# Turning float64 weights into float32 by scaling and shifting, and loading the first of them first

## The chip, the core and the metric

The kernel runs on one core of a Trainium2 chip. A core has five engines that work side by side, each with an instruction queue of its own that it works off in order: TensorE (PE in the profile; its weight loads are PEld) multiplies matrices into PSUM, VectorE (DVE) and ScalarE (ACT) do elementwise work, GpSimd (POOL) does elementwise work on SBUF, and SyncE (SP) here only issues DMA transfers. The metric is device time in microseconds, the median of several executions. Everything here is one core, one launch.

## The reference, cut to what matters

```python
# B, H, S, D = 8, 8, 576, 64; window 128
scores = q @ k^T / 8 + slope[h] * -(i - j)        # only for 0 <= i - j < 128, otherwise -1e9
attn   = softmax(scores);  x = attn @ v           # x: [8, 576, 512], heads side by side
theta  = x @ w_theta
zr, zi = x * cos(theta), x * sin(theta)
y      = w_tok_r @ zr + w_tok_i @ zi              # over the 576 tokens
u      = x + y
out    = u + max(u @ w_ch, 0)
```

q, k and v are float32. The weights w_theta, w_tok_r, w_tok_i and w_ch are float64: float32 draws divided by the square root of a dimension, which gives numbers of double precision. [...] A float64 has 1 sign bit, 11 exponent bits and 52 mantissa bits; the high word holds the sign, the exponent and the first 20 mantissa bits, the low word the other 32.

## The kernel before, in words

**Batches.** Everything is done batch by batch. For one batch (8 heads, handled as 4 pairs of heads) `attend` computes the windowed attention into `x_sb`, `turn` transposes x and computes theta, its cosine and sine and the products z, `mix` multiplies z with the token weights (wtok, 27 matmuls for each of 8 output pieces, line L536), and `channels` multiplies u with w_ch (L557) and writes the output. The attention of batch b+1 runs beside the mixing of batch b, which is what keeps TensorE busy in the long middle of the kernel. Products that need more precision than TensorE gives in one pass are done as a high part and a low part (`kh`/`kl`, `qh`/`ql`, `wth_hi`/`wth_lo`, `wtk_hi`/`wtk_lo`, `wch_hi`/`wch_lo`).

**The first stage.** Batch 0's attention has no mixing beside it. It is done by `start`, which also loads and converts all weights: 4 blocks of w_theta (512 columns), 9 blocks of the token weights (576 columns) and 4 blocks of w_ch (512 columns), 17 in all, each [128, columns] of float64. Its loop has five turns; in turn p it makes the scores of pair p (`Pair.scores`, L351 and L365 on TensorE, L380 on VectorE, the exponent L383 on ScalarE) and finishes pair p-1: `flip` transposes the scores (L388) and copies them (L391), `values` multiplies them with v (L424), `finish` divides (L430 to L433). `fill` issues matmuls whose results nobody reads (L569). `prepare(p)` splits q and k of pair p-1 into high and low parts (`split_pair`: kh L300 and qh L297 on ScalarE, ql L298 on VectorE, kl L301 on GpSimd) and loads pair p. `head.ready()` loads v for four heads at the first of them (`load_plain`, L218, 650 KB), and `measure_first` (L276 on VectorE) takes the largest |v| of such a group.

**The weights.** `unpack` is a generator: each `next` issues one stage of one block, and `pace` calls it three times for every five steps of the scores; what is left is issued after the loop. A block's stages are: `load` (L139) into one of four buffers (two of `big`, two of `uf`), `apart`, `together`, `split`. A buffer is taken again when its block has been split. `apart` masks the high word into the exponent bits (L149) and into the mantissa bits with the hidden one (L151), both on VectorE, and ScalarE's Relu turns the exponent bits into those of a float32 power of two (L153). `together` puts the sign on the power (L158), adds the low word times 2^-32 to the mantissa as a float32 (L160), both on VectorE, and GpSimd multiplies the two (L162). For token weights it also takes the sum of absolute values of each row (L165 on ScalarE) and a power of two from it (L166, L121, L123). `split` writes the scaled high part on ScalarE (L175, L179, L182) and the low part on VectorE (L176, L183) or GpSimd (L180).

**What sets the order.** The order of the instructions on each engine isn't the order of the code: when the kernel is built, a planner times all instructions with a model of its own and places them by priority, which is mostly the order in which the code issues them, as soon as its model says that their inputs and buffers are there. Some streams get other priorities (`urgent`, with MIX, CHAN and ROTATE) and some instructions are tied behind others (`issue_after`). The order found is then fixed; on the chip each engine works its own list off in order and waits where an input isn't there yet. All DMA transfers of this kernel are issued from SP's list.

At the end of `start`, `scales_first` computes scales for z from the row sums and the largest |v|; then pair 4's scores are made, and `turn` of batch 0 begins.

Of the kernel before, what the change touches and what calls it, by code (L numbers as in the profile page):

```python
# [11 lines left out]
F32 = mybir.dt.float32  # L12
F32R = mybir.dt.float32r
I32 = mybir.dt.int32
U32 = mybir.dt.uint32
F16 = mybir.dt.float16
BF16 = mybir.dt.bfloat16
AF = mybir.ActivationFunctionType
ALU = mybir.AluOpType
# [30 lines left out]
def attn_moe_kernel(ctx: ExitStack, tc: tile.TileContext, qt, kt, vx, wth, wtok, wch, band, out):  # L50
    nc = tc.nc
    PSUM = bass.MemoryType.PSUM

    const = ctx.enter_context(tc.tile_pool(name="const", bufs=1))
# [37 lines left out]
    scales = fixed[:, 130:134]  # L92
    bands = const.tile([128, 704], F32, name="bands")
    bnd = bands[:, :256]
    rebias = const.tile([128, 1], F32, name="rebias")
    make_identity(nc, ident)
    nc.vector.memset(halfpi, math.pi / 2)
    nc.sync.dma_start(out=bands, in_=band)
    nc.vector.memset(ones, 1.0)

    for g in range(H // 2):
# [7 lines left out]
    wtk_lo = const.tile([128, 9, S], F16, name="wtk_lo")  # L109
    sums, rows, invs, lim = (rings[name].take() for name in ("sum", "row", "inv", "lim"))  # L110

    nc.vector.memset(rebias, -float(916 << 23))
    qr = const.tile([128, S + 64], F32, name="qr")
    for t in [qr] + peaks + lasts:
        nc.gpsimd.memset(t, 0.0)
# [15 lines left out]
    def unpack(jobs, places):  # L131
# [10 lines left out]
        def words(k, t):  # L142
            w = jobs[k][4]
            raw = t[:, :2 * w].rearrange("p (n t) -> p n t", t=2)
            return raw, t[:, 2 * S:2 * S + w], t[:, 3 * S:3 * S + w]

        def apart(k, t):
            raw, ex, ma = words(k, t)
            nc.vector.tensor_scalar(out=ex, in0=raw[:, :, 1], scalar1=0x7FF00000, scalar2=None,  # L149
                                    op0=ALU.bitwise_and)  # L150
            nc.vector.tensor_scalar(out=ma, in0=raw[:, :, 1], scalar1=0xFFFFF, scalar2=0x100000,  # L151
                                    op0=ALU.bitwise_and, op1=ALU.bitwise_or)
            nc.scalar.activation(ex, ex, AF.Relu, bias=rebias, scale=8.0)  # L153

        def together(k, t):
            raw, ex, ma = words(k, t)
            val = ma.bitcast(F32)
            nc.vector.scalar_tensor_tensor(out=ex, in0=raw[:, :, 1], scalar=-0x80000000, in1=ex,  # L158
                                           op0=ALU.bitwise_and, op1=ALU.bitwise_or)
            nc.vector.scalar_tensor_tensor(out=val, in0=raw[:, :, 0].bitcast(U32), scalar=2.0 ** -32, in1=ma,  # L160
                                           op0=ALU.mult, op1=ALU.add)
            nc.gpsimd.tensor_tensor(out=val, in0=val, in1=ex.bitcast(F32), op=ALU.mult)  # L162
            if jobs[k][5] == "row":
                c = jobs[k][3]
                nc.scalar.activation(ex.bitcast(F32), val, AF.Abs, accum_out=sums[:, c:c + 1])  # L165
                nc.vector.tensor_scalar(out=sums[:, c:c + 1], in0=sums[:, c:c + 1], scalar1=2.0 ** -100, scalar2=None,  # L166
                                        op0=ALU.max)
                power(rows[:, c:c + 1], sums[:, c:c + 1], WEXP)
# [404 lines left out]
    raw, parts = {}, {}  # L573

    def prepare(p):

        if 0 <= p - 1 < pairs and p - 1 not in parts:
            parts[p - 1] = split_pair(p - 1, raw.pop(p - 1))
        if p < pairs and p not in raw:
            raw[p] = load_pair(p)  # L580
# [54 lines left out]
    def start(x_sb, load):  # L635
# [6 lines left out]
                if paces[0] * 3 % 5 < 3:  # L642
                    next(load, None)

        for p in range(2):
            prepare(p)
        last = None
        for p in range(H // 2 + 1):
            new = Pair(p) if p < H // 2 else None
            if new is not None:  # L650
                for head in new.heads:
                    head.ready()
            if new is not None and p % 2 == 0:
                measure_first(p // 2)
            if p == 3:
                load_values(2)

# [19 lines left out]
            else:  # L677
                for tiles in SCORES:
                    scores(tiles)
            if new is not None:  # L680
                prepare(p + 2)
            last = new
        for _ in load:
# [105 lines left out]
```

## Time and profile before

| | |
|---|---|
| median of 3 runs | 770.2 us (770.09 to 770.59) |
| the profiled execution | 770.52 us, span 768.7 us |
| busy in the span: TensorE, its weight loads | 703.3 us (91%), 579.9 us (75%) |
| busy: VectorE, ScalarE, GpSimd | 570.4 (74%), 478.9 (62%), 215.6 us (28%) |
| first mixing matmul (L536) | at 130.7 us |
| weight loads L139 on SP | first issued at 4.15 us, last at 90.48 us |

The page gives busy time by engine and the span in 40 slices of 19.2 us, each digit a share of busy time in tenths. A row of the timeline is start, duration, engine, line, operation, output<-inputs, shapes, count and, in brackets, how long the engine had been idle and for what. A row of the windows table is a stretch, its length, and the busy time (with the number of instructions) of each engine, then TensorE's granted clock as a share of full speed, the share of busy DMA engines and GB/s; where it is asked for one line of the code, only that line's engine is shown. "Chain of waits" is the work that ended last, followed back step by step.

### The profile page before, as it was taken

The page shows a single profiled execution, that of the slowest core. Times are in us where ns is not written, and L with a number is a line of the kernel's source. Part 1 is how long each engine was busy: PE and PEld are TensorE (multiplying, and loading weights), DVE is VectorE, ACT ScalarE, POOL GpSimd, SP SyncE. Part 2 cuts the span into 40 slices and gives each one's busy share as a digit, 9 for nine tenths or more (in the row PEclk, how much of TensorE's full clock was granted, in tenths as well). Part 3 has the DMA queues.
Part 4 walks back from the last instruction along what each step waited for, and adds up shares of the span by engine and source line. Part 5 has one row for each costly group of instructions (what it writes and reads, how often), then busy time and mean ns, then how long its engine had stood idle before and what let it go on. Part 6 is the DMA issues. An engine that isn't in the chain of part 4 may idle for free.

```text
span 768.7 us, 16184 instructions
## 1 busy us (share of the span) xinstructions
PE 703.3 (91%) x6218; PEld 579.9 (75%) x6221; DVE 570.4 (74%) x1554; ACT 478.9 (62%) x948; POOL 215.6 (28%) x249
## 2 busy tenths in 40 slices
PE   3777588999999999989999999999999999999998
PEld 2466476778878887778878887788778887788777
DVE  5999888888579847797579847887579857864722
ACT  3678638856678547774678647774678547844610
POOL 3343524321233105212232204221233105211420
PEclk8678569999999999999999999999999999999999
DMA  7544220312112200321012301321012200100101
GB/s 259 155 154 152 87 65 2 88 46 64 39 55 81 84 32 32 96 55 60 24 55 72 93 32 32 97 68 48 24 55 82 82 32 32 33 2 32 32 1 62
DMA packets 32621, 49.87 MB, mean 65 GB/s; under 512 B 5664, under 2 KB 22048, under 8 KB 32544
## 3 DMA queue, kind: packets, MB, share of 16 engines
q1 hardware_dynamic: 32544, 48.84, 20.8%
q8 instruction: 49, 0.80, 0.4%
q14 instruction: 28, 0.23, 0.1%
HBM read 39.39 MB, written 9.44 MB: 64 GB/s over the span
## 4 chain that ended last, share of the span: by engine, by line
PE 45%; DVE 29%; ACT 15%; DMA 7%; issue 3%; POOL 0%; SPq 0%; DVEq 0%; ACTq 0%; POOLq 0%
PE mm L536 16%; PE mm L557 7%; PE mm L475 6%; DMA vb<-in_vx_dram 5%; PE s_ps L365 5%; PE t_ps L388 5%; PE acc L424 5%; DVE f L490 4%; ACT s_sb L383 3%; DVE g L492 3%; DVE s_sb L380 2%; DVE g L500 2%; ACT f L489 2%; ACT g L496 2%; DVE pt L396 2%
## 5 line engine op out<-in xcount | busy, mean ns | idle before, releaser
L536 PE MATMUL mm<-wtk_hi,z_hi 128*128 128x288 f16 x576 | 161.9, 288 | 6.1 <-DVE f L487 3.6
L536 PE MATMUL mm<-wtk_lo,z_hi 128*128 128x288 f16 x576 | 161.3, 288 | 0.0
L536 PE MATMUL mm<-wtk_hi,z_lo 128*128 128x288 f16 x576 | 158.8, 287 | 0.0
L536 PEld LDWEIGHTS <-z_hi 128*128 128x128 f16 x1152 | 108.9, 98 | 36.3 <-issue 6.7
L383 ACT ACTIVATE s_sb<-s_sb,fixed 128x256 f32<-128x256 f32 (+1 forms) x256 | 102.1, 469 | 16.8 <-DVE fixed L380 16.7
L544 POOL TENSOR_TENSOR u_lo<-xtf,u_hi 128x288 fp32r<-128x288 f32 x64 | 51.8, 816 | 195.1 <-ACT u_hi L543 178.9
L380 DVE CUSTOM_DVE_ANT_0 s_sb<-s_ps,bands 128x256 f32<-128x256 f32 (+1 forms) x256 | 85.1, 383 | 1.3 <-PE s_ps L365 1.3
L396 DVE SCALAR_TENSOR_TENSOR pt<-t_ps,pt 128x512 f16<-128x512 f32 x112 | 75.9, 685 | 10.5 <-ACT pt L395 10.5
L388 PE MATMUL t_ps<-fixed,s_sb 128*128 128x128 f32 x448 | 77.3, 289 | 6.4 <-ACT s_sb L383 2.0
L395 ACT ACTIVATE pt<-t_ps 128x512 f16<-128x512 f32 x112 | 65.2, 588 | 25.0 <-PE t_ps L388 24.4
L447 POOL TENSOR_TENSOR z_lo<-g,z_hi 128x512 f16<-128x512 f32 x32 | 37.7, 1177 | 134.8 <-ACT z_hi L446 134.8
L301 POOL TENSOR_TENSOR kl<-kr,kh 128x576 fp32r<-128x576 f32 x32 | 50.2, 1569 | 64.3 <-ACT kh L300 64.3
L424 PE MATMUL acc<-vh,pt 128*128 128x65 f16 x1008 | 65.7, 195 | 1.9 <-DVE x_sb L433 1.8
L536 PEld LDWEIGHTS <-z_lo 128*128 128x128 f16 x576 | 57.1, 99 | 13.6
L424 PEld LDWEIGHTS <-pt 128*128 128x128 f16 x1512 | 59.8, 98 | 9.8 <-DVE x_sb L433 2.3
L388 PEld LDWEIGHTS t_ps<-fixed,s_sb 128*128 128x128 f32 x448 | 53.6, 148 | 14.5 <-ACT s_sb L383 6.0
L543 ACT CAST u_hi<-xtf 128x288 fp32r<-128x288 f32 x64 | 27.1, 427 | 59.1 <-DVE xtf L541 58.9
L424 PE MATMUL acc<-vl,pt 128*128 128x64 f16 x504 | 56.3, 193 | 0.0
L557 PE MATMUL mm<-u_hi,wch_hi 128*128 128x288 f32 x256 | 53.0, 321 | 1.3 <-DVE xtf L560 1.1
L496 ACT ACTIVATE g<-g,fixed 128x512 f32<-128x512 f32 (+1 forms) x40 | 29.0, 725 | 39.7 <-DVE g L492 39.2
L365 PE MATMUL s_ps<-kh,qh 64*128 64x256 f32 (+1 forms) x256 | 48.9, 344 | 5.1 <-DVE fixed L380 4.5
L475 PE MATMUL mm<-wth_hi,x_hi 128*128 128x512 f32 x160 | 46.0, 409 | 7.9 <-DVE f L490 7.3
(146 smaller groups left out, 1598.4 us busy)
## 6 DMA issues: line engine op xcount, KB each, us to landing
vb<-in_vx_dram SPq DMA_DIRECT2D x16, 650.0 KB, 4.2
kr<-in_kt_dram SPq DMA_DIRECT2D x32, 288.0 KB, 2.9
out_dram<-xtf SPq DMA_DIRECT2D x64, 144.0 KB, 1.8
qr<-in_qt_dram SPq DMA_DIRECT2D x32, 144.0 KB, 2.7
qr<-in_qt_dram SPq DMA_DIRECT2D x32, 128.0 KB, 2.8
xtf<-in_wtok_dram SPq DMA_DIRECT2D x4, 576.0 KB, 5.0
u_hi<-in_wtok_dram SPq DMA_DIRECT2D x3, 576.0 KB, 3.8
u_lo<-in_wtok_dram SPq DMA_DIRECT2D x2, 576.0 KB, 4.4
```

The source lines that it names most:

```text
L301: nc.gpsimd.tensor_tensor(out=kl, in0=kr, in1=kh.bitcast(F32), op=ALU.subtract)
L365: nc.tensor.matmul(ps[:, e, off:off + kn], qm[rows, q0:q0 + qn], km[rows, k0:k0 + kn], start=(j == 0), stop=(j == last))
L380: nc.vector.tensor_tensor_reduce(out=sb, in0=ps, in1=bias, scale=2.0 ** -(2 * self.p % H + 1), scalar=3.0e38, op0=ALU.add, op1=ALU.min, ac ...
L383: self.exp = nc.scalar.activation(sb, sb, AF.Exp, bias=least, scale=-1.0)
L388: nc.tensor.transpose(t_ps[:, 128 * n:128 * n + 128], self.sc[i, e][:, 128 * j:128 * j + 128], ident)
L395: nc.scalar.activation(pt[:, 0], t_ps, AF.Copy, scale=2.0 ** PEXP)
L396: nc.vector.scalar_tensor_tensor(out=pt[:, 1], in0=t_ps, scalar=2.0 ** PEXP, in1=pt[:, 0], op0=ALU.mult, op1=ALU.subtract)
L424: nc.tensor.matmul(av[:, i, :r.shape[-1]], l, r, start=(n == 0), stop=(n == len(prods) - 1))
L475: nc.tensor.matmul(t_ps, a[:, c * 128:c * 128 + 128], w[:, c, :], start=(k == 0 and c == 0), stop=(k == len(prods) - 1 and c == 3))
L536: nc.tensor.matmul(y_ps[:, :HALF], z[:, c, m * 128:m * 128 + 128], w[:, c, cs], start=(k == 0), stop=(k == 26))
L544: nc.gpsimd.tensor_tensor(out=u_lo[:, m, cs], in0=xtf[:, m, cs], in1=u_hi[:, m, cs].bitcast(F32), op=ALU.subtract)
L557: nc.tensor.matmul(o_ps[:, :HALF], w[:, c, e * 128:e * 128 + 128], u[:, c, cs], start=(k == 0), stop=(k == 11))
```

## The change

The conversion uses other arithmetic. The high word, read as a float32, has the same sign bit; its 8 exponent bits are the first 8 of the 11, and its mantissa starts with the last 3. Multiplied by 2^-112 (ScalarE, Copy with a scale) it keeps its mantissa and its exponent bits lose 112, which for numbers of this size leaves the upper three at zero. Shifted left by 3 as an integer, the last 3 exponent bits join the exponent and the sign falls out; the freed three bits are filled with the top three bits of the low word (shifted right by 29), and the sign is put back from the scaled word. So a block takes, in place of two masks, Relu, two two-input operations and the GpSimd product: one ScalarE Copy, one VectorE shift and two VectorE two-input operations. The constant `rebias` goes. The result is the float64 cut off at 24 bits.

The order in `start` changes too: the first weight block's load and `apart` are issued ahead of pair 0's q and k; `bands` (the table of biases that the scores add, and the input of `fill`) is loaded behind pair 0's loads instead of first of all; and `head.ready()` (with the load of v) and `measure_first` come after the scores and products of a turn, `measure_first` in the odd turns instead of the even ones.

```diff
     bands = const.tile([128, 704], F32, name="bands")
     bnd = bands[:, :256]
-    rebias = const.tile([128, 1], F32, name="rebias")
     make_identity(nc, ident)
     nc.vector.memset(halfpi, math.pi / 2)
-    nc.sync.dma_start(out=bands, in_=band)
     nc.vector.memset(ones, 1.0)
...
-    nc.vector.memset(rebias, -float(916 << 23))
...
         def apart(k, t):
-            raw, ex, ma = words(k, t)
-            nc.vector.tensor_scalar(out=ex, in0=raw[:, :, 1], scalar1=0x7FF00000, scalar2=None,
-                                    op0=ALU.bitwise_and)
-            nc.vector.tensor_scalar(out=ma, in0=raw[:, :, 1], scalar1=0xFFFFF, scalar2=0x100000,
-                                    op0=ALU.bitwise_and, op1=ALU.bitwise_or)
-            nc.scalar.activation(ex, ex, AF.Relu, bias=rebias, scale=8.0)
+            raw, z, b = words(k, t)
+            nc.scalar.activation(z.bitcast(F32), raw[:, :, 1].bitcast(F32), AF.Copy, scale=2.0 ** -112)
 
         def together(k, t):
-            raw, ex, ma = words(k, t)
-            val = ma.bitcast(F32)
-            nc.vector.scalar_tensor_tensor(out=ex, in0=raw[:, :, 1], scalar=-0x80000000, in1=ex,
+            raw, z, b = words(k, t)
+            val = b.bitcast(F32)
+            nc.vector.tensor_scalar(out=b, in0=z, scalar1=3, scalar2=None, op0=ALU.logical_shift_left)
+            nc.vector.scalar_tensor_tensor(out=b, in0=raw[:, :, 0], scalar=29, in1=b,
+                                           op0=ALU.logical_shift_right, op1=ALU.bitwise_or)
+            nc.vector.scalar_tensor_tensor(out=b, in0=z, scalar=-0x80000000, in1=b,
                                            op0=ALU.bitwise_and, op1=ALU.bitwise_or)
-            nc.vector.scalar_tensor_tensor(out=val, in0=raw[:, :, 0].bitcast(U32), scalar=2.0 ** -32, in1=ma,
-                                           op0=ALU.mult, op1=ALU.add)
-            nc.gpsimd.tensor_tensor(out=val, in0=val, in1=ex.bitcast(F32), op=ALU.mult)
+            ex = z
             if jobs[k][5] == "row":
...
-        for p in range(2):
-            prepare(p)
+        next(load)
+        prepare(0)
+        nc.sync.dma_start(out=bands, in_=band)
+        prepare(1)
         last = None
         for p in range(H // 2 + 1):
             new = Pair(p) if p < H // 2 else None
-            if new is not None:
-                for head in new.heads:
-                    head.ready()
-            if new is not None and p % 2 == 0:
-                measure_first(p // 2)
             if p == 3:
                 load_values(2)
...
             if new is not None:
+                for head in new.heads:
+                    head.ready()
+                if p % 2:
+                    measure_first(p // 2)
                 prepare(p + 2)
             last = new
```

## The prediction

> **What bounds the kernel now.** I read the head of the page first, then a table of stretches, then the timelines of VectorE, GpSimd and TensorE inside the first stretch. The head:
>
> ```profile
> span 768.7 us, 16184 instructions
> ...
> PE   3777588999999999989999999999999999999998
> ...
> DVE  5999888888579847797579847887579857864722
> ```
>
> Over most of the 40 slices (19.2 us each) TensorE (PE) is the full engine, but slices 1 to 5 are different: there VectorE (DVE) is full and TensorE is not. The stretches, with columns busy time and count of TensorE, its weight loads, VectorE, ScalarE, GpSimd, then granted clock, DMA share, GB/s:
>
> ```profile
> 0.00:10.00 10.00, 2.73 (x8) 1.31 (x9) 1.30 (x9) 2.78 (x3) 3.79 (x14) 1.00 0.78 257
> 10.00:95.00 85.00, 58.87 (x354) 44.21 (x354) 79.74 (x221) 58.58 (x118) 34.58 (x23) 0.71 0.48 152
> 95.00:104.00 9.00, 6.05 (x26) 5.69 (x27) 7.56 (x26) 1.34 (x2) 2.59 (x3) 0.50 0.00 0
> 104.00:131.00 27.00, 23.75 (x151) 19.81 (x150) 22.35 (x53) 20.25 (x38) 7.17 (x7) 0.88 0.16 48
> 131.00:768.70 637.70, 611.93 (x5685) 508.86 (x5683) 459.43 (x1251) 395.90 (x788) 167.42 (x203) 1.00 0.17 52
> ```
>
> From 10 to 95 us VectorE works 79.74 of 85 us; nothing else is above 70%, and the granted clock of TensorE is 0.71. From 131 us on TensorE works 611.93 of 637.70 us (96%). All that the change edits runs before 104 us, so the question is how much earlier the first stage ends; the rest is a block of some 638 us that should move with it.
>
> **The change part by part. (a) VectorE's instructions.** Before, each of the 17 blocks of weights (8 of 512 columns, 9 of 576) takes two one-input masks (L149, L151) and two two-input operations (L158, L160) on VectorE, a Relu on ScalarE (L153) and a product on GpSimd (L162). Busy time of each line from 0 to 104 us, in the order L149, L151, L160, L158, L162, L153, and kl's split L301:
>
> ```profile
> 0.00:104.00 104.00, 9.30 (x17) 0.72 0.47 149
> 0.00:104.00 104.00, 11.97 (x17) 0.72 0.47 149
> 0.00:104.00 104.00, 14.10 (x17) 0.72 0.47 149
> 0.00:104.00 104.00, 14.12 (x17) 0.72 0.47 149
> 0.00:104.00 104.00, 26.57 (x17) 0.72 0.47 149
> 0.00:104.00 104.00, 12.69 (x17) 0.72 0.47 149
> 0.00:104.00 104.00, 7.03 (x5) 0.72 0.47 149
> ```
>
> The four VectorE lines sum to 49.5 us. Single instructions of the timeline (start, duration) show what one costs when left alone, and what it costs beside GpSimd:
>
> ```profile
> 11.22 0.42 DVE L149 TENSOR_SCALAR u_hi<-u_hi 128x512 int32<-128x512 int32 x1
> ```
>
> ```profile
> 12.62 0.68 DVE L158 SCALAR_TENSOR_TENSOR u_hi<-u_hi 128x512 int32<-128x512 int32 x1
> ```
>
> ```profile
> 42.79 2.02 DVE L298 SCALAR_TENSOR_TENSOR ql<-qr,fixed,qh 128x640 fp32r<-128x640 f32 x1
> 44.87 1.82 DVE L176 SCALAR_TENSOR_TENSOR wtk_lo<-u_hi,fixed,wtk_hi 128x576 f16<-128x576 f32 x1
> ```
>
> ```profile
> 53.33 0.76 DVE L158 SCALAR_TENSOR_TENSOR u_hi<-u_hi 128x576 int32<-128x576 int32 x1
> 54.00 0.46 DVE L149 TENSOR_SCALAR u_lo<-u_lo 128x576 int32<-128x576 int32 x1
> 54.37 1.68 DVE L151 TENSOR_SCALAR u_lo<-u_lo 128x576 int32<-128x576 int32 x1
> 56.04 1.69 DVE L149 TENSOR_SCALAR xtf<-xtf 128x576 int32<-128x576 int32 x1
> ```
>
> ```profile
> 42.16 3.91 POOL L162 TENSOR_TENSOR xtf<-xtf 128x576 f32<-128x576 f32 x2 [1.38 <-DVE fixed L123]
> ```
>
> ```profile
> 54.22 1.50 POOL L162 TENSOR_TENSOR u_hi<-u_hi 128x576 f32<-128x576 f32 x1 [8.15 <-issue]
> 56.01 1.40 POOL L301 TENSOR_TENSOR kl<-kr,kh 128x576 fp32r<-128x576 f32 x1 [0.29 <-ACT kh L300]
> ```
>
> Alone, a mask takes 0.42 (512 columns) or 0.46 us, a two-input operation 0.68 or 0.76. The mask at 54.37 takes 1.68: it ends just after GpSimd's product (54.22 to 55.72). Likewise ql at 42.79 and wtk_lo at 44.87, beside the two products from 42.16 to 46.07. So the product costs VectorE time as well as GpSimd's.
>
> Undisturbed, the four lines would take 8 x (2 x 0.42 + 2 x 0.68) + 9 x (2 x 0.46 + 2 x 0.76) = 39.6 us; the other 9.9 us of the 49.5 are such waits. After the change a block has on VectorE one one-input shift (z << 3) and two two-input operations. The shift reads and writes contiguous words; the nearest row below is the mask (0.42/0.46), above the two-input 0.68/0.76 (if a shift had not the mask's rate: 17 x 0.28 = 4.8 us worse). I take the mask, also a one-input integer operation out of and into the same memory. The two-input pair takes what L158 takes, being of its form and strides. One mask per block goes; as an instruction starts 0.09 us before the end of the one ahead (54.00 + 0.46 against 54.37), that is 17 x 0.35 = 6.0 us. Of the 9.9 us of waits I let 2.6 stay, since kl's split remains (the mask at 56.04, 1.69 us, loses 1.2 us to it) and so do the four wch_lo subtractions: 7.3 gone. ql goes back from 2.02 to 0.88, its median in the row below, and wtk_lo from 1.82 to the 0.76 of the other two-input operations of that width, 2.2 us. Together **-15.5 us** of VectorE time.
>
> ```profile
> L298 DVE SCALAR_TENSOR_TENSOR ql<-qr,fixed,qh x32: 870/878/2024, 7.3 to 667.4; 128x640 fp32r<-128x640 f32 x32
> ```
>
> The page SBUF — State Buffer of the Trainium skill, in its section on the two sides of the memory, states a rule that speaks against part of this: the ports shared by VectorE and GpSimd are an exclusive lock, taken by any VectorE operation in its doubled rate or with two inputs there, and the loser blocks for the other's whole instruction. By that rule all three new VectorE operations still block against kl's split, 7.03 us in all, where I let 2.6 stay: the sum would be some 4.4 us smaller. The rows above agree with the lock itself (1.68 against 0.46); how often the pair meets only the new order decides.
>
> **(b) ScalarE and GpSimd.** ScalarE's Relu (12.69 us, 0.75 each) becomes a Copy with a fixed scale from every second word; the nearest rows are Relu itself above and, below, the scaled Copy that splits wth (512 columns):
>
> ```profile
> 14.80 0.63 ACT L182 ACTIVATE wth_hi<-u_hi 128x512 fp32r<-128x512 f32 x1 [0.40 <-POOL u_hi L162]
> ```
>
> That is 0 to at most -2.0 us (17 x 0.12) on an engine with room (58.58 of 85 us): I take 0. GpSimd loses 26.57 us that weigh only through VectorE, counted above; a block's way is also shorter by a product, which lets its buffer, one of four, be reloaded sooner.
>
> **(c) The order at the start.** The first weight block is issued ahead of pair 0's q and k, bands behind those, vb behind pair 0's scores, and the peak measurements (L276) come after pairs 1 and 3. Now:
>
> ```profile
> 0.74 0.39 SPq L98 DMA_DIRECT2D bands<-in_band_dram  x1
> ```
>
> ```profile
> 9.82 1.49 DVE L276 TENSOR_REDUCE peak<-vb 128x4 f32<-128x1280 f32 x1 [1.68 <-DMA vb<-in_vx_dram]
> ```
>
> ```profile
> u_hi<-in_wch_dram SPq DMA_DIRECT2D x1, 512.0 KB, 4.0
> ```
>
> VectorE stands waiting for vb until 9.82 with the weights' first mask (11.22) behind it. Issued at 0.74 and landing in 4.0 us, as a lone block of that size does, the first block is on ScalarE near 4.8 and on VectorE near 5.5. Against that, k and q come later by one issue (0.4 us) and by the 512 KB in front of them, 1 to 2 us by the rate of 257 GB/s in the first stretch, and only the first weight block is early; the two measurements still cost VectorE 1.49 each. Bounds: 0 (the other blocks land as late as now) and 11.22 - 5.5 = -5.7. I take **-3 us**. vb is covered, since pair 0's first product with it is at 25.8; bands, used first by the matmuls that only keep TensorE's clock up (L569, at 8.1), has some 1 to 3 us less room:
>
> ```profile
> 8.14 4.00 PE L569 MATMUL mm<-bands,fixed 128*128 128x512 bf16 x10
> ```
>
> ```profile
> 15.69 0.35 DVE L380 CUSTOM_DVE_ANT_0 last<-mm,bands 128x192 f32<-128x192 f32 x1
> ```
>
> ```profile
> 25.76 1.00 PE L424 MATMUL acc<-vb,pt 128*128 128x65 f32 x8
> ```
>
> Its other cover is VectorE, which comes to its first scores at 15.7, behind the weights; without these covers the first pair would lose what they are late, once, up to 3 us.
>
> **(d) What is late next.** VectorE's 79.74 of 85 leave 5.3 us idle. With 15.5 us less on VectorE, TensorE's 58.87 and ScalarE's 58.58 us stand in 70 us and not 85, so VectorE will wait for them more often. Bounds: 0 and some 9 (its idle share tripled); I take **+3**. Sum: -15.5 - 3 + 3 = -15.5 us. The profiled execution took 770.52 us for its span of 768.7 (1.8 around it), like the median of 770.2; 770.5 - 15.5 = **755.0 us**.
>
> **The rivals.** (1) *The tail gains too.* VectorE, an in-order queue, waits there for the last block, and TensorE behind it:
>
> ```profile
> 94.58 0.43 DVE L149 TENSOR_SCALAR u_hi<-u_hi 128x512 int32<-128x512 int32 x1 [2.75 <-DMA u_hi<-in_wch_dram]
> ```
>
> ```profile
> 74.27 2.19 PE L424 MATMUL acc<-vb,pt 128*128 128x65 f32 x18 [1.10 <-DVE x_sb L433]
> ```
>
> ```profile
> 97.87 0.59 PE L249 MATMUL mm<-fixed 128*128 128x9 f32 x2 [7.25 <-DVE fixed L247]
> ```
>
> ```profile
> 99.02 4.07 PE L424 MATMUL acc<-vb,pt 128*128 128x65 f32 x18
> ```
>
> If the blocks are through before, the 2.75 us go, and TensorE, not idle for 7.25 us, does the last head's products in 2.19 and not 4.07 us (granted clock 0.50 in that stretch): 4.6 more, near 750, and 745 if (c) and (d) also come out at their good ends. Against: the last block is always loaded into the buffer of the fifth from last. The page TensorE: Matmul & The Clock Gate of the Trainium skill (Part 1) states that an idle window of about 3.4 us halves this clock; the two rows above agree. (2) *The pairs' own chain binds*: scores, exponent, transposes and products of one pair follow one another over VectorE, ScalarE and TensorE, and a TensorE that waits stays at the low clock (0.71 on average). Then about half the gain is left: 763. For it: TensorE is already 69% busy; against it: VectorE's 94%. (3) *Slower: ScalarE waits for transfers.* The instruction that waits for a weight block moves from VectorE's queue to ScalarE's, where exponents and copies out of PSUM queue behind it, and TensorE behind those. 13 of the 17 loads wait for a buffer and land 4.0 us after; if each holds ScalarE for more than 18.5/13 = 1.4 us all is lost, at 2 us each it is 26 - 18.5 = +7.5: 778. Against it: before, VectorE shows only one such wait above 1 us, the 2.75 above. (4) *The stage gains but the planned order of the later 638 us changes for the worse*; TensorE's 96% there leaves place for 1%, 6 us either way.
>
> **How the numbers follow.** Forecast, 750 to 761: 0.57. Tail gain, 742 to 750: 0.15. Chain binds or the later order takes part, 761 to 768.5: 0.18. No change that can be told, within 0.2% (what a measurement of this kernel can tell): 0.02. ScalarE's waits, above 772: 0.08. So faster 0.90, same 0.02, slower 0.08. A range of 744 to 764 leaves out the far ends of the second and third and all of the last, about 0.2.
>
> **What would show it.** Right: the two-input weight operations and ql near 0.7 to 0.9 us with few above 1; the shift at 0.42 to 0.46; no GpSimd product; VectorE's first weight work near 5.5 us; the first mixing products 13 to 18 us ahead of where they are now. Wrong: a shift at 0.7; long ScalarE waits for weight transfers with TensorE idle; VectorE below 80% in the first stage with the same end; or a later stage longer by more than 3 us.

## The result, and the profile after

The changed kernel takes 763.4 us (759.4 to 767.1, nine executions), the kernel before 770.1 (768.4 to 772.0): a ratio of 0.9905 with a 95% interval of 0.988 to 0.993. It is faster, by 6.7 us where 15.5 were forecast; the time lies in the range, near its upper end. The profiled execution is the shortest of the nine (759.4 us, span 757.5). The head of its page, then the stretches with the columns of the table shown for the kernel before:

```profile
span 757.5 us, 16151 instructions
...
PE   4788987999999999899999999999999999999998
...
DVE  6998768777779758786679757886679857864722
```

```profile
0.00:10.00 10.00, 1.85 (x6) 1.01 (x7) 3.89 (x12) 4.63 (x6) 4.10 (x14) 1.00 0.80 272
10.00:95.00 85.00, 71.82 (x462) 53.94 (x460) 76.35 (x241) 62.30 (x129) 12.99 (x11) 0.78 0.53 163
95.00:117.00 22.00, 17.91 (x73) 13.93 (x72) 15.30 (x33) 14.51 (x27) 5.44 (x5) 0.84 0.02 6
117.00:757.50 640.50, 614.47 (x5686) 510.00 (x5683) 459.64 (x1252) 396.63 (x789) 167.55 (x203) 1.00 0.17 52
```

The first stage is shorter: of its first six slices VectorE is the fuller engine in 1 to 3 only, in slice 4 both have the digit 8, and in slices 5 and 6 TensorE is ahead (9 and 8 against 7 and 6). In slice 7, where the mixing begins, it is 7 against 8. The mixing begins at 116.8 us in place of 130.7, and what follows takes 640.7 us in place of 638.0:

```profile
116.76 0.28 PE L530 MATMUL mm<-wtk_hi,z_hi 128*128 128x288 f16 x1 [0.97 <-DVE fixed L374]
```

The conversion itself did what it was forecast to do. VectorE's weight work is now three lines, the shift (L151) and two two-input operations (L152, L154). Their busy time to 104 us, in that order, and the first of them in the timeline:

```profile
0.00:104.00 104.00, 8.52 (x17) 0.79 0.51 161
0.00:104.00 104.00, 13.47 (x17) 0.79 0.51 161
0.00:104.00 104.00, 12.22 (x17) 0.79 0.51 161
```

```profile
5.42 0.43 DVE L151 TENSOR_SCALAR u_hi<-u_hi 128x512 int32<-128x512 int32 x1 [4.41 <-ACT u_hi L146]
5.88 0.69 DVE L152 SCALAR_TENSOR_TENSOR u_hi<-u_hi 128x512 int32<-128x512 int32 x1
```

They sum to 34.2 us, where the four lines of before took 49.5. What stands out is the end of the stage on TensorE: of the products of heads 5 to 7 (L418) those of head 5 take 3.94 us where the same 18 matmuls of head 6 take 2.19, so that TensorE is at half clock there (called cold below), and there is a wait for x_lo, which VectorE makes only after it has waited for the last load of v (L230):

```profile
77.93 3.94 PE L418 MATMUL acc<-vb,pt 128*128 128x65 f32 x18
...
85.25 2.19 PE L418 MATMUL acc<-vb,pt 128*128 128x65 f32 x18 [0.32 <-DVE x_sb L427]
...
99.60 2.08 PE L469 MATMUL mm<-wth_hi,x_lo 128*128 128x512 f32 x4 [2.96 <-DVE x_lo L461]
```

```profile
96.09 1.49 DVE L230 TENSOR_REDUCE peak<-vb 128x4 f32<-128x1280 f32 x1 [1.81 <-DMA vb<-in_vx_dram]
```

### The profile page after: what moved, and what is told of

The parts are those of the page before. It is cut to its first block, busy times and chain, and to the rows that moved or that the text cites. A ratio compares the mean times of both kernels' runs of the same rounds, so it can differ in the third digit from the quotient of the medians.

```text
span 757.5 us, 16151 instructions
## 1 busy us (share of the span) xinstructions
PE 706.1 (93%) x6221; PEld 578.9 (76%) x6221; DVE 555.2 (73%) x1536; ACT 478.1 (63%) x948; POOL 190.1 (25%) x232
## 4 chain that ended last, share of the span: by engine, by line
PE 48%; DVE 24%; ACT 16%; DMA 8%; issue 3%; POOL 0%; ACTq 0%; SPq 0%; DVEq 0%; POOLq 0%
PE mm L530 16%; PE mm L551 7%; PE mm L469 6%; PE acc L418 6%; PE s_ps L359 5%; PE t_ps L382 5%; DMA vb<-in_vx_dram 5%; DVE f L484 4%; ACT s_sb L377 4%; DVE g L486 3%; DVE g L494 2%; ACT g L490 2%; ACT f L483 2%; DVE s_sb L374 2%; DVE ql L292 2%
## 5 line engine op out<-in xcount | busy, mean ns | idle before, releaser
L418 PE MATMUL acc<-vh,pt 128*128 128x65 f16 x1008 | 65.2, 195 | 0.0
L418 PEld LDWEIGHTS <-pt 128*128 128x128 f16 x1512 | 59.4, 98 | 7.3
L418 PE MATMUL acc<-vl,pt 128*128 128x64 f16 x504 | 56.0, 194 | 0.0
```

What stands on the lines that cost most here:

```text
L418: nc.tensor.matmul(av[:, i, :r.shape[-1]], l, r, start=(n == 0), stop=(n == len(prods) - 1))
```

## The experiments

All were timed against the kernel before on the same chip, whose median there lay between 769.5 and 770.9 us. They are shown in the order in which they were run. Where a diff is given "to the changed kernel" or "to the new conversion alone", the other edits are as there.

**The whole change again, and its two halves.** `a1_after` is the changed kernel. `a2_arith` has the new conversion, in the order of before; `a3_order` the new order, with the conversion of before.

> The changed kernel again, beside the three others on one chip. Both theories: 763.4 us as first measured, single executions from 759 to 767. Theory 2 (the first stage is now bound by the pairs' chain over a TensorE that is often at its low clock) expects the long executions to be those with the lower mean granted clock; theory 1 (VectorE still binds) expects no tie between clock and time.

> The new conversion alone, in the old order of the loads and measurements. Theory 1 (VectorE's time sets the first stage, so its 15.5 us count in full but for what other engines take): 770.1 - 15.5 + 3 = 757.6, and the gap of the changed kernel to the forecast comes from its order. Theory 2 (freed VectorE time runs into the pairs' chain on TensorE and ScalarE): 763 to 767, no better than the whole change.

> The old conversion in the new order (first weight block first, bands behind pair 0, v and the measurements behind the scores). Theory 1: VectorE is full from 10 to 95 us, so starting its work earlier pays: 770.1 - 3 = 767. Theory 2 says the same here, as VectorE is as loaded as before. If the order by itself costs time (a v that lands late in the tail), it is at or above 770.

| | median us | ratio to before |
|---|---|---|
| a1_after | 764.4 (759.5 to 767.7) | 0.992 [0.989, 0.995] |
| a2_arith | 754.3 (750.0 to 755.3) | 0.978 [0.976, 0.981] |
| a3_order | 777.8 (776.1 to 778.7) | 1.009 [1.0075, 1.011] |

The new conversion alone gains 15.9 us, as much as the whole forecast; the new order alone loses 7.6, and on top of the new conversion it loses 9 to 10. The step that failed is the order. As for the tie of time and clock that `a1_after` asks for: of the 15 executions of the changed kernel the three shortest (759.4 to 759.8) have a mean granted clock of 0.968 to 0.971, the two longest (767.1 and 767.7) 0.960; between them the tie is loose (764.7 at 0.968, 764.1 at 0.955).

**The product put back.** To the changed kernel, one product on GpSimd per block whose result nobody reads (it goes over the raw words, which are not needed any more).

```diff
                                            op0=ALU.bitwise_and, op1=ALU.bitwise_or)
+            nc.gpsimd.tensor_tensor(out=t[:, :jobs[k][4]].bitcast(F32), in0=val, in1=val, op=ALU.mult)
             ex = z
```

> The changed kernel plus one GpSimd product per block of weights, of the old size and at the old place, whose result nobody reads (it goes over the raw words), so the shared ports see the old traffic without the old arithmetic. Theory 1: the waits beside the product (7.3 us in the four weight lines, 2.2 us elsewhere) come back on an engine that sets the time: 763.4 + 9 = 772. Theory 2: VectorE has room for them: 764 to 767.

Measured: 769.6 us (764.0 to 772.6), ratio 0.9986 [0.9966, 1.0005], so 5.2 us over the changed kernel beside it, between the two expectations. The product is worth about half of the 9.5 us of waits that step (a) laid to it, within a plan that the added instructions move as well.

**The order in two halves.** Both to the new conversion alone. `b1_block_first` has the first block's load and first stage ahead of pair 0 and `bands` behind it; `b2_v_behind` has `head.ready()` and the measurement (odd turns) behind a turn's scores.

```diff
-    nc.sync.dma_start(out=bands, in_=band)
...
-        for p in range(2):
-            prepare(p)
+        next(load)
+        prepare(0)
+        nc.sync.dma_start(out=bands, in_=band)
+        prepare(1)
```

```diff
-            if new is not None:
-                for head in new.heads:
-                    head.ready()
-            if new is not None and p % 2 == 0:
-                measure_first(p // 2)
...
             if new is not None:
+                for head in new.heads:
+                    head.ready()
+                if p % 2:
+                    measure_first(p // 2)
                 prepare(p + 2)
```

> The new conversion with one half of the new order: the first weight block's load and first stage ahead of pair 0, and bands behind pair 0's loads. v and its measurements stay at the head of each turn, as before the change. Measured so far: new conversion alone 754.3 us, with the whole new order 763.4 to 764.4 us. Theory 1, the 9 to 10 us come from v: its loads and measurements behind the scores make heads 5 to 7 and the last load of v late; then this kernel takes 750 to 756 us (the early block was forecast to give up to 3). Theory 2, the loss comes from the start, where bands and q, k stand behind the first 512 KB: 761 to 765 us. Theory 3, the two halves share it, since each edit shifts the planned order of the whole first stage a little: 757 to 760 us.

> The new conversion with the other half of the new order: v is loaded behind the scores of a turn and measured after the odd turns; bands and pair 0 are loaded first, as before the change. Theory 1, the loss comes from v: 762 to 766 us, with the turn's first product 3 us or more later than the 91.5 us of the new conversion alone. Theory 2, the loss comes from the start: 753 to 756 us. Theory 3, both share it: 757 to 760 us.

Measured: 756.5 us (754.3 to 760.0), ratio 0.982 [0.979, 0.985], and 769.2 us (767.0 to 772.9), ratio 0.998 [0.997, 0.9996]. The half that moves v makes the loss, 14.9 us, more than any of its expectations; beside a v that goes ahead, the early block gives nothing and may cost some 2 us. Beside a v that goes behind, it gains: the changed kernel is `b2_v_behind` with the early block and the later `bands`, and takes 763.4 to 764.4 us where that takes 769.2.

**A third buffer for v**, in the changed kernel and in the new conversion alone (`vbp` with 3 buffers in place of 2), against the wait for the last load of v that the profile after shows.

> The changed kernel with a third buffer for v, so that no load of v waits for a buffer. In the changed kernel the load for the third group of heads is issued at 91.9 us, VectorE waits 1.8 us for it, and TensorE stands idle 2.96 us with cold products behind. Theory 1, this wait at the end of the first stage carries a part of the loss: 2 to 5 us less than the changed kernel, 758 to 762 us, with no wait for v after 90 us. Theory 2, the loss is made earlier, by the order of heads 5 to 7, and something else is late in its place: 762 to 766 us.

> The new conversion in the old order, with a third buffer for v. The new conversion alone took 754.3 us. Theory 1 (the wait for v's buffer matters wherever the conversion is fast): 750 to 753 us. Theory 2 (in the old order v is loaded early enough, the third buffer changes nothing but the planned order): 752 to 757 us.

Measured: 763.9 us (761.9 to 765.2) and 756.5 us (754.8 to 757.1). The first does not say what the wait is worth, since the third buffer did not take it away: with `b3_three_v` the load is issued at 92.24 us (91.86 in the changed kernel), right behind a pair's q and k, and VectorE waits longer for it, 3.74 us in place of 1.81:

```profile
96.74 1.49 DVE L230 TENSOR_REDUCE peak<-vb 128x4 f32<-128x1280 f32 x1 [3.74 <-DMA vb<-in_vx_dram]
```

What it is worth is seen from other traces. `b1_block_first`, and `e2_v_ahead` and `e3_weights_back` further below, wait 1.59, 1.53 and 2.90 us at this place and take 756.5, 758.7 and 758.2 us; so the late load of v, well visible as it is, does not make the 5 to 8 us by which these are faster than the changed kernel. The new conversion alone has no such wait, so it may be a part of what is left between them and its 754.3.

**The measurement or the load.** To the new conversion alone: `c1_measure_odd` has only the measurements in the odd turns, `c2_v_behind_even` has the loads behind the scores and the measurement right behind them in the even turns.

```diff
-            if new is not None and p % 2 == 0:
+            if new is not None and p % 2:
                 measure_first(p // 2)
```

> The new conversion in the old order, with one thing of the new order: the two measurements of v come in the odd turns instead of the even ones; v is still loaded ahead of a turn's scores. So far: new conversion alone 754.3 us, with v loaded and measured behind the scores 769.2 us. Theory 1, the later measurements make the loss (they stand on VectorE ahead of the next pair's work): 764 to 769 us. Theory 2, the later load of v makes it, since the planned order then puts heads' products behind the next pair's scores: 753 to 757 us here.

> The new conversion, with v loaded behind a turn's scores, and measured right there in the even turns. Theory 1 (later measurements make the loss): 754 to 758 us. Theory 2 (the later load of v makes it): 764 to 770 us. Theory 3, neither as such: any edit of this kind gives another planned order of TensorE and ScalarE in the first stage, and the time goes with how early the heads' products stand in it; then this run can land anywhere from 754 to 770 us, and the end of head 3's products (57.6 us in the new conversion alone, 64.9 in the changed kernel, 74.7 with v behind) tells the time: per us of it, some 0.8 us of the whole.

Measured: 754.3 us (753.2 to 756.9), ratio 0.979, and 769.9 us (768.4 to 772.0), ratio 1.000 [0.9986, 1.0015]. The loads make it, the measurements nothing. Against the third theory, that an edit of this kind can land anywhere from 754 to 770 us: the four kernels up to here that have the new conversion and load v ahead of the scores take 754.3 to 756.5 us (`a2_arith`, `b1_block_first`, `b4_arith_three_v`, `c1_measure_odd`), the two that load it behind, with the start as before, 769.2 and 769.9.

**More and fewer matmuls without readers.** `c3_fill_late`: to the changed kernel, six more of them ahead of each head's products in the last two turns. `c4_no_fill`: the changed kernel without any.

```diff
                 last.flip(2)
+                if p >= 3:
+                    fill(6)
                 one.values()
                 one.finish(x_sb)
                 last.flip(3)
                 scores(SCORES[2])
+                if p >= 3:
+                    fill(6)
                 two.values()
```

> The changed kernel with 24 more of the matmuls whose results nobody reads, in the last two turns of the first stage, ahead of the heads' products there. In the changed kernel the products of heads 5 to 7 take 3.94, 2.19 or 4.07, and 2.13 or 3.94 us in two executions of the same program, as TensorE's granted clock is 0.5 or 1 there. Theory 1, the half clock between 76 and 97 us carries a part of the loss and of the spread: 2 to 5 us less, 759 to 762 us, with less spread. Theory 2, the extra matmuls themselves (24 by 0.21 to 0.42 us, 5 to 10 us) stand in the chain, and the clock falls again behind them: 766 to 772 us.

> The changed kernel without the 40 matmuls whose results nobody reads (about 4 us of TensorE in each turn). Theory 1, TensorE's queue now binds the first stage, and these matmuls stand ahead of the heads' products: 3 to 10 us less, 753 to 761 us. Theory 2, they only use time in which TensorE would wait, and keep its clock up: without them the granted clock of the first stage falls from 0.75 and the time rises by 2 to 8 us, 766 to 772 us.

Measured: 761.9 us (761.6 to 763.3), at the edge of what its first theory expected, and 761.5 us (760.0 to 767.6), between its two. Both are about 2 us below the changed kernel, which is less than its own executions differ by; so TensorE's clock at the end and the matmuls in its queue are each a small term at most.

**One load.** To the new conversion alone, only the load of v for pairs 0 and 1 (group 0, 650 KB) is issued behind pair 0's scores, and its measurement with it; that for pairs 2 and 3 stays ahead.

```diff
-            if new is not None:
+            if new is not None and p >= 2:
                 for head in new.heads:
                     head.ready()
-            if new is not None and p % 2 == 0:
-                measure_first(p // 2)
+                if p % 2 == 0:
+                    measure_first(p // 2)
...
             if new is not None:
+                if p < 2:
+                    for head in new.heads:
+                        head.ready()
+                    if p % 2 == 0:
+                        measure_first(p // 2)
                 prepare(p + 2)
```

> The new conversion in the old order, with one load moved: v of the first four heads is loaded (and measured) behind pair 0's scores; v of the next four stays ahead of pair 2's. In SP's list three weight loads then stand ahead of this one load, where none did. Theory 1, this one load makes the whole loss: 767 to 771 us. Theory 2, the second load makes it (it comes nearer to its use): 754 to 757 us. Theory 3, each makes a part: 760 to 764 us.

Measured: 769.7 us (766.1 to 772.8), ratio 0.9997 [0.998, 1.0013]: the place of this one load (the measurement alone cost nothing in `c1_measure_odd`) is worth 15.4 us, nearly the whole gain of the conversion. SP's list at the start, where it now stands behind three weight blocks:

```profile
2.87 0.60 SPq L207 DMA_DIRECT2D qr<-in_qt_dram  x1
3.51 0.59 SPq L139 DMA_DIRECT2D u_hi<-in_wth_dram  x1
4.14 0.43 SPq L139 DMA_DIRECT2D u_lo<-in_wth_dram  x1
4.61 0.43 SPq L139 DMA_DIRECT2D xtf<-in_wth_dram  x1
5.09 0.43 SPq L215 DMA_DIRECT2D vb<-in_vx_dram  x1
```

It is issued 1.57 us later than in the new conversion alone (3.52 us), and no product on TensorE waits for v in either trace. What it moves is the rest of the order. Some 36 us on, the load of a token block stands behind pair 3's three loads of q, where it stood ahead of them; ScalarE waits for it, and a copy of transposed scores (L388) queues behind the wait, with TensorE behind the copy. With `e1_group0`, SP, ScalarE and TensorE:

```profile
41.11 0.58 SPq L139 DMA_DIRECT2D u_lo<-in_wtok_dram  x1
```

```profile
47.52 0.72 ACT L149 ACTIVATE u_lo<-u_lo 128x576 f32<-128x576 f32 x1 [4.39 <-DMA u_lo<-in_wtok_dram]
48.15 0.57 ACT L388 COPY pt<-t_ps 128x512 f32<-128x512 f32 x1
```

```profile
48.77 1.11 PE L385 MATMUL t_ps<-fixed,s_sb 128*128 128x128 f32 x4 [2.56 <-ACT pt L388]
51.19 0.69 PE L385 MATMUL t_ps<-fixed,last 128*128 128x128 f32 x2 [1.30 <-ACT pt L388]
53.38 4.11 PE L421 MATMUL acc<-vb,pt 128*128 128x65 f32 x18
```

The new conversion alone, SP and ScalarE at the same place:

```profile
39.53 0.42 SPq L139 DMA_DIRECT2D u_lo<-in_wtok_dram  x1
```

```profile
43.78 1.05 ACT L388 COPY pt<-t_ps 128x512 f32<-128x512 f32 x2
45.46 0.73 ACT L149 ACTIVATE u_lo<-u_lo 128x576 f32<-128x576 f32 x1 [0.63 <-DMA u_lo<-in_wtok_dram]
```

The wait is 4.39 us against 0.63, TensorE stands 2.56 and 1.30 us, and head 2's products, cold behind that, take 4.11. This place is not the whole of it: `b1_block_first` has this load behind the loads of q as well (issued at 40.64 us), waits 2.65 us for it, and takes 756.5 us:

```profile
44.91 0.72 ACT L148 ACTIVATE u_lo<-u_lo 128x576 f32<-128x576 f32 x1 [2.65 <-DMA u_lo<-in_wtok_dram]
```

**v's place put back, in two ways.** `e2_v_ahead` is the changed kernel with `head.ready()` back at the head of a turn, all else as changed. `e3_weights_back` is the changed kernel, but the weights' loads and stages are planned at a lower priority than the pairs' work.

```diff
-    start(x_sb, unpack(JOBS + LATE, ((big, "u_hi"), (big, "u_lo"), (uf, "xtf"), (uf, "xtf"))))
+    start(x_sb, urgent(unpack(JOBS + LATE, ((big, "u_hi"), (big, "u_lo"), (uf, "xtf"), (uf, "xtf"))), -60))
```

> The changed kernel with the loads of v back ahead of the scores; the first weight block first, bands behind pair 0's loads, and the measurements in the odd turns stay. Theory 1, the place of v's load is all of the loss: 754 to 758 us, like the new conversion alone and with the first block first (754.3 and 756.5). Theory 2, the parts of the order cost together what none costs alone: 761 to 765 us.

> The changed kernel, all of it, with the weights' loads and stages planned at a lower priority (60 places) than the pairs' work; nothing else is moved. In SP's list the first load of v then stands ahead of the weights again, although the code still issues it behind pair 0's scores; the first weight block stands behind it. Theory 1, what counts is the place of v's load against the weights' loads in SP's list, and the planned order of the other engines that follows from it: 753 to 758 us. Theory 2, the late place in the code costs in another way (v's buffer, the measurements): 762 to 766 us.

Measured: 758.7 us (757.6 to 760.1), ratio 0.985 [0.983, 0.987], and 758.2 us (757.4 to 759.2), ratio 0.985 [0.983, 0.987]. Both recover 5 to 6 of the 9 to 10 us, a little less than the theory of v's place expected. In the second the code still issues v behind the scores, but in SP's list it goes ahead of the weights:

```profile
2.87 0.60 SPq L204 DMA_DIRECT2D qr<-in_qt_dram  x1
3.51 0.59 SPq L212 DMA_DIRECT2D vb<-in_vx_dram  x1
4.14 0.50 SPq L136 DMA_DIRECT2D u_hi<-in_wth_dram  x1
```

That fits v's place against the weights' loads as what counts, not its place in the code; but this edit also puts the first weight block behind pair 0's loads again and moves the weights' stages on every engine, so it does not show the place by itself. The other 4 us of `e2_v_ahead` stay with the first block and `bands`: it is `b1_block_first` with the measurements in the odd turns (nothing, by `c1_measure_odd`), and takes 758.7 us where that takes 756.5.

**The matmuls without readers in the good order.** To the new conversion alone: the 24 further ones of `c3_fill_late`, none at all, and 5 in place of 10.

> The new conversion in the old order, with the 24 further matmuls whose results nobody reads, in the last two turns of the first stage. In the changed kernel they gave 761.9 us in place of 763.4 to 764.4, with a smaller spread. In the new conversion alone, head 7's products take 4.07 us at half clock from 80.6 us, behind a wait of TensorE of 2.57 us. Theory 1, the half clock costs here too: 750 to 753 us. Theory 2, the extra matmuls stand in the way as much as they help: 753 to 757 us.

> The new conversion in the old order, without the 40 matmuls whose results nobody reads. Theory 1, with a short conversion TensorE's queue is what the pairs wait for, and these matmuls stand in it: 745 to 752 us. Theory 2, they fill idle time and keep the clock up, and without them the granted clock of the first stage falls below 0.78: 756 to 764 us. Theory 3, both cancel, as in the changed kernel (2 us less): 752 to 756 us.

> The new conversion in the old order, with 5 in place of 10 of these matmuls in each turn. Theory 1: half of f1's gain, 749 to 753 us. Theory 2: 754 to 759 us. Theory 3: 752 to 756 us.

Measured: 760.7 us (758.2 to 761.6), 754.5 (750.5 to 759.2) and 756.9 (752.9 to 759.1), against 754.3. More of them cost 6 us, above both expectations; leaving them out neither costs nor gives. None of the kernels run has a lower median than the new conversion in the old order, which beats both the kernel before and the changed one, with 754.3 us.

**Where the stage loses it.** For some of the kernels, by their traces: the time at which VectorE ends the division of heads 1, 3 and 7 (the start of its last step), the start of the mixing, and the span behind that.

| | median | head 1 | head 3 | head 7 | mixing | behind it |
|---|---|---|---|---|---|---|
| before | 770.1 | 46.8 | 68.9 | 103.6 | 130.7 | 638.0 |
| new conversion alone (a2) | 754.3 | 40.3 | 57.6 | 85.1 | 112.8 | 635.4 |
| measurement moved too (c1) | 754.3 | 40.4 | 58.6 | 86.2 | 113.5 | 639.7 |
| first block first (b1) | 756.5 | 47.1 | 58.8 | 91.0 | 116.0 | 641.9 |
| changed | 763.4 | 47.6 | 64.9 | 92.3 | 116.8 | 640.7 |
| changed, second trace (a1) | 764.4 | 47.4 | 64.8 | 97.2 | 120.3 | 639.5 |
| one load behind (e1) | 769.7 | 51.4 | 66.9 | 98.0 | 129.0 | 639.1 |

At head 1 the changed kernel is 7 us behind the new conversion alone. There the order on TensorE differs: the new conversion alone has head 1's products ahead of the matmuls without readers,

```profile
35.09 2.19 PE L421 MATMUL acc<-vb,pt 128*128 128x65 f32 x18
...
38.53 2.33 PE L566 MATMUL mm<-bands,fixed 128*128 128x512 bf16 x10
```

and the changed kernel has them behind these; then pair 1's transposes wait for a copy on ScalarE that stands behind a weight block, and head 2's products are cold:

```profile
36.92 4.02 PE L563 MATMUL mm<-bands,fixed 128*128 128x512 bf16 x10
...
42.26 2.22 PE L418 MATMUL acc<-vb,pt 128*128 128x65 f32 x18
...
47.09 0.68 PE L382 MATMUL t_ps<-fixed,s_sb 128*128 128x128 f32 x4 [1.95 <-ACT pt L385]
...
49.76 3.94 PE L418 MATMUL acc<-vb,pt 128*128 128x65 f32 x18
```

```profile
44.51 0.72 ACT L146 ACTIVATE xtf<-xtf 128x576 f32<-128x576 f32 x1 [0.77 <-DMA xtf<-in_wtok_dram]
...
46.47 1.05 ACT L385 COPY pt<-t_ps 128x512 f32<-128x512 f32 x2
```

This picture alone does not make the loss. `b1_block_first` has it too and is as late at head 1 (47.1 us):

```profile
37.46 3.56 PE L565 MATMUL mm<-bands,fixed 128*128 128x512 bf16 x9 [0.33 <-issue]
40.85 2.12 PE L420 MATMUL acc<-vb,pt 128*128 128x65 f32 x18
...
46.82 0.78 PE L384 MATMUL t_ps<-fixed,s_sb 128*128 128x128 f32 x4 [1.84 <-ACT pt L387]
47.59 4.10 PE L420 MATMUL acc<-vb,pt 128*128 128x65 f32 x18
...
54.21 4.08 PE L420 MATMUL acc<-vb,pt 128*128 128x65 f32 x18
```

Yet its median is 756.5 us, and `c4_no_fill`, early at head 1 (37.1 us), takes 761.5. It is at head 3 that the kernels of the table stand in the order of their medians. There `b1_block_first` is at 58.8 us, with head 3's products (54.21) ahead of the next matmuls without readers, and the changed kernel at 64.9, with ten of these (54.62, 3.90 us long) ahead of head 3's products (59.86). Outside the table this is no rule either (`c4_no_fill` is at 57.7), and no run changes this place by itself.

By the table, of the 9 to 10 us, some 5.4 lie ahead of the mixing (118.5 on the mean of the two traces of the changed kernel, 113.1 of a2 and c1) and some 2.6 behind it (640.1 against 637.5). The traces are single executions, and not the median ones: 759.4 and 762.1 us for the changed kernel with its median of 764, 750.0 and 755.0 for a2 and c1 with 754.3, and 760.0, the longest of its five, for b1.

## Why the prediction was right in its main term and wrong in its sum

That the time lies in the range is luck: the conversion gained the whole 15.5 us by itself, and a step put down as a gain of 3 us lost 9 to 10. The mixing, expected 13 to 18 us earlier, came 13.9 and 10.4 us earlier in the two traces of the changed kernel, and 17.9 with the new conversion alone.

**(a) VectorE's instructions: right.** The four lines fell by 15.3 us of busy time where 13.3 were forecast; the removed mask counts here with its whole 0.44 us, in the forecast with the 0.35 by which the next instruction starts earlier. Undisturbed, the three lines would take 8 x 1.80 + 9 x 1.95 = 32.0 us (0.42 or 0.45 for the shift, 0.69 or 0.75 for each of the others), so 2.2 us of waits stayed where I let 2.6 stay. The shift runs at the mask's rate, as chosen. The wait beside kl's split is still there, on single instructions (GpSimd, then VectorE, of the changed kernel):

```profile
50.65 1.40 POOL L295 TENSOR_TENSOR kl<-kr,kh 128x576 fp32r<-128x576 f32 x1 [13.29 <-ACT kh L294]
```

```profile
50.85 1.52 DVE L151 TENSOR_SCALAR xtf<-xtf 128x576 int32<-128x576 int32 x1
```

The shift takes 1.52 us in place of 0.45. These rows agree with the lock that the Trainium skill states (SBUF — State Buffer, on the two separate sides), but the estimate made from it, that all 7 us of kl's split stay as waits, was too large in this order. What did not come is ql: 7.30 us for 6 of them, 1.2 each (5.53 for 5, 1.1 each, before), where 0.88 was forecast, and kl's split still runs beside it; wtk_lo fell from 8.35 to 7.29 us for its nine.

**(b) ScalarE and GpSimd: right as far as it went.** The Copy takes 0.66 or 0.72 us. That the instruction which waits for a block now stands in ScalarE's list was named under the third rival, and not in the sum.

**(c) The order at the start, -3 us with bounds of 0 and -5.7: this is the step that failed.** Its visible part came true: the first weight work on VectorE is at 5.42 us, forecast 5.5. But the step's bounds left out a loss, and it measured +7.6 us alone (a3) and +9 to +10 on top of the new conversion. The sentence that fell is "vb is covered, since pair 0's first product with it is at 25.8". The transfer is covered indeed: no instruction of pair 0 or 1 waits for it. But the place of the load has a second effect, which I had put at nothing: other loads change places with it, and the order planned for all engines changes too. By `e1_group0` that place alone is worth 15.4 us, by `e2_v_ahead` and `e3_weights_back` 5 to 6 of the changed kernel's 9 to 10; the parts do not add. The early block, for which the -3 stood, has both signs: some +2 us where v goes ahead (`b1_block_first` against `a2_arith`), -5 to -6 where it goes behind (the changed kernel against `b2_v_behind`).

**(d) What is late next, +3: too dear.** The new conversion alone gains 15.9 us where (a) and (d) gave 12.5. With (a) a little under its 15.5, that leaves nothing for (d), or a gain of the tail against it.

**The rivals.** The second (the pairs' chain binds, or the later order takes part, 763 us at 0.18) has the time, and half of the mechanism: by the traces TensorE waits for the pairs' copies after some 40 us, but in an order that came with the edit, and the new conversion alone shows that this need not cost the gain. The first (the tail gains too): VectorE's wait of 2.75 us for the last block became one of 1.61 us on ScalarE in the changed kernel and is gone in the new conversion alone, and there the 7.25 us of idle TensorE shrank to 2.57, with the products still cold at 4.07; the row:

```profile
80.58 4.07 PE L421 MATMUL acc<-vb,pt 128*128 128x65 f32 x18 [2.57 <-DVE fixed L123]
```

The third (ScalarE waits for transfers) did not decide the changed kernel: from 15 us on these waits are 1.58, 0.43, 0.77, 0.18, 1.44 and 1.61 us, 6.0 in all, of which the new conversion alone has 4.6. It is however how the loss looks where it is largest, with 4.39 us in one place (`e1_group0`). The fourth (the later 638 us): the span behind the start of the mixing moved by -2.6 to +3.9 us over the traces of the table, and by +1.5 and +2.7 in the two of the changed kernel.

**What stays open.** That the place of v's load makes the loss is shown. Whether it does so by the order that the planner builds on it or by the changed times of the transfers themselves is only argued from the traces: list and order came together in each kernel, and one with the loads of one and the computing order of the other was not run. Nor is it shown which of the first block and `bands` makes the other 4 us, nor why the two halves of the order do not add.

## What to carry to other kernels

Where a planner fixes the order of all engines, price a moved load by more than its own arrival: ask which transfers overtake it in the issuing queue, and treat the order that follows as a term of its own with both signs, here 5 to 15 us, as large as the arithmetic that was the change. If a change joins a new computation with a new order, time the two apart: here the computation alone was the better kernel. And a wait that stands out at the end of a stage (the late v) need not be the cause, nor the first place at which two traces part (head 1, 45 us earlier): ask a third kernel that has the same wait or the same place, and look in its trace whether an edit took the wait away at all.

## What the hardware showed that was not expected

Two executions of the changed kernel run alike to 84 us, within 0.7 us, and part there by TensorE's clock alone: the one shown above has head 6's products at full speed (2.19 us at 85.25), the other, same program, at half, and head 7's too:

```profile
84.60 4.07 PE L418 MATMUL acc<-vb,pt 128*128 128x65 f32 x18 [0.32 <-DVE x_sb L427]
...
92.76 3.94 PE L418 MATMUL acc<-vb,pt 128*128 128x65 f32 x18
```

Its mixing starts 3.5 us later for it (120.3 against 116.8). The Trainium skill (TensorE: Matmul & The Clock Gate, Part 1) says that the window by which the clock is granted runs freely and is not tied to the kernel; the two traces agree with that, though no row shows the window itself. And the matmuls without readers, which hold that clock up, are worth nothing here that can be told: without them the granted clock from 10 to 95 us falls to 0.66 in the changed kernel (0.78 and 0.72 in its two traces) and to 0.72 from 0.76 in the new conversion alone, and the time stays where it was or is 2 us less.
